# Value copies of the dilated attention: one feature to a DMA issue in place of two

## The chip, the core and the metric

The kernel runs on one core of a Trainium2 chip. A core has five engines that run side by side, each with its own queue of instructions in a fixed order: TensorE (PE, matrix products; its weight loads are shown as PEld), VectorE (DVE), ScalarE (ACT), GpSimd (POOL) and SyncE (SP). In this kernel SP's queue issues nearly all DMA transfers, which are carried out by 16 DMA engines. The metric is the time of one execution on the device, in microseconds; of several runs the median is given.

## What is computed

Four layers follow each other on x, of 2048 rows and 512 columns in bf16: A, B, A, B. Each is `x = x + layer(layernorm(x))`, with 32 heads of 16 features. The A layers are a linear attention with a softmax feature map. The B layers are a sliding attention in which row s looks at the eight rows s, s-2, ..., s-14:

```python
qkv = (x @ wqkv).reshape(B, S, 3, H, Dh)            # H = 32, Dh = 16
idx = pos[:, None] - off[None, :]                   # off = 0, 2, ..., 14
kg, vg = k[:, :, idx_c, :], v[:, :, idx_c, :]       # eight keys and values for each row
logits = einsum("bhsd,hswd->bhsw", q, kg) * Dh ** -0.5   # rows before the start masked
attn = softmax(logits)
o = einsum("bhsw,bhswd->bhsd", attn, vg)
return o.reshape(B, S, D) @ wo
```

The change concerns `vg` in the B layers: how the values reach the engine that multiplies them by `attn`.

## The kernel before

The rows are cut into four blocks of 512. What is called layer 0 and layer 1 below (L in the names) is a pair A, B each, so that there are eight B blocks (two layers of four). Work is recorded as small steps (`step`, L174) under a name of stage and engine. A list written out in the kernel (`_ORDER`, L56) then emits one step after another, so every engine's instructions stand in an order fixed by hand; no scheduler moves them. Buffers come from pools whose slots are written out as well: Vg, prod, pav and Ek share eight large buffers ("big"), so a transfer into one of them may have to wait until an earlier user is done.

One B block goes like this:

- `s_b1` (L919) projects q, k and v with TensorE (L927); ScalarE or VectorE moves the results out of PSUM (L191). The columns of the weight are taken four apart, so partition 4h + dl holds the features 4 dl to 4 dl + 3 of head h, one in each of four chunks of 16 + 512 rows, the 16 being the rows before the block. Such a group of four is what is called one feature below (dl, or q where it is used: 0 to 3). GpSimd fills those 16 (L965, L969).
- `vwr` (L971 to L973) writes V to DRAM, one row of 4 x 528 elements for each of the 128 partitions: row 4h + dl is feature dl of head h.
- `vrep` reads it back four times, shifted: partition 32g + h of Vg receives the row of head h from position 2 + 2g on, 2104 elements of 2 bytes. So the four groups g of 32 partitions hold four of the eight offsets, and the other four are read 8 elements further on. Vg consists of two tiles, k = 0 with dl = 0 and 1, k = 1 with dl = 2 and 3.
- `s_b2` forms the products of q and k on VectorE (prod, L1015), sums them on TensorE (L1022), and makes the softmax: E (L1029), its sum (L1038), its reciprocal (L1043, L1045) and the weights PT (L1050).
- `s_b3` (L1064) takes the features in turn: for q = 0 to 3 VectorE multiplies PT by the window of Vg of feature q (pav, L1077: tile q // 2, half q % 2), TensorE adds over the offsets (L1086), and the sum is moved to oT (L191). In the last two blocks of layer 1 the product of q = 3 is made in two halves of columns.
- `s_out` (L508) multiplies oT by the output weights (L519), adds x (L522 with L529 on ScalarE, or L532 on VectorE), and goes on to the next norm, whose result xn is transposed into xnT, in most blocks by a DMA (L450) on SP's queue.

In each B block SP's queue so has one write of V (vd, L973) and four steps of `vrep`, of two DMAs each. The steps lie at places of their own in the order, with transposes and other blocks' writes between some of them. In the first half of each tile's transfer the groups 0 and 2 come, in the second the groups 1 and 3. The last two blocks of layer 1 are interleaved: both of block 3's steps for k = 0, one of block 2's, both of block 3's for k = 1, and then the other three of block 2's.

A DMA completes on one of eight semaphores, given out in turn; an issue waits until the DMA that had the same one, eight DMAs before, has landed. A pav waits for the DMAs that wrote what it reads.

Of the kernel before, what the change touches and what calls it, by code (L numbers as in the profile page):

```python
# [19 lines left out]
H = 32  # L20
# [3 lines left out]
NB = 4  # L24
# [5 lines left out]
KVW = 16 + TB  # L30
VGW = 3 * KVW + TB + 8
# [97 lines left out]
class _Fast:  # L129
# [789 lines left out]
    def s_b1(self, L, b):  # L919
        nc, add = self.nc, self.step  # L920
        st = "b1_%d%d" % (L, b)
        T = {}
        def mm(i, c):
            xnT = self.xnT["B%d" % L, b]
            T[i, c] = pp = self.ps()
            for k in range(NB):
                nc.tensor.matmul(pp[:], lhsT=self.WB[:, k, i * D + c:(i + 1) * D:NB], rhs=xnT[:, :, k, :],  # L927
                                 start=(k == 0), stop=(k == NB - 1))

        def ev(i, c, dve):  # L930
            if i == 0:
                if (L, b) not in self.QT:
                    self.QT[L, b] = self.med([NB, TB], "QT")
                dst = self.QT[L, b][:, c, :]
            elif i == 1:
                ktile()
                dst = self.K[L, b][:, c, 16:KVW]
            else:
                vtile()
                dst = T["V"][:, c, 16:KVW]  # L940
            self.copy(dve, dst, T[i, c][:])

        def ktile():
            if (L, b) not in self.K:
                self.K[L, b] = self.med([NB, KVW], "K")

        def vtile():
            if "V" not in T:
                T["V"] = self.med([NB, KVW], "V")

        def halo():
            ktile()
            nc.gpsimd.tensor_copy(out=self.K[L, b][:, :, 0:16], in_=self.K[L, b - 1][:, :, TB:KVW])

        def kzero():
            ktile()
            nc.gpsimd.memset(self.K[L, b][:, :, 0:16], 0.0)

        def vzero():
            vtile()  # L960
            nc.gpsimd.memset(T["V"][:, :, 0:16], 0.0)

        def vhalo_in():
            vtile()
            nc.gpsimd.tensor_copy(out=T["V"][:, :, 0:16], in_=self.vh[L, b - 1][:])  # L965

        def vhalo_out():
            self.vh[L, b] = self.sm([NB, 16], "vh", BF16)
            nc.gpsimd.tensor_copy(out=self.vh[L, b][:], in_=T["V"][:, :, TB:KVW])  # L969

        def vwr():  # L971
            self.VD[L, b] = self.dram.tile([P, NB * KVW], BF16, name="vd%d%d" % (L, b))
            nc.sync.dma_start(out=self.VD[L, b][:], in_=T["V"][:].rearrange("p c t -> p (c t)"))  # L973

        def vrep(k, gs):
            if gs[0] == 0:
                if k == 0:
                    self.Vg[L, b] = {}
                self.Vg[L, b][k] = self.big([2, NB * KVW], "Vg")
            n = NB * KVW  # L980
            for g in gs:
                a = self.VD[L, b][2 * k:2 * k + 1, 2 + 2 * g:3 + 2 * g]
                src = bass.AP(a.tensor, a.offset, [[4 * n, H], [n, 2], [1, VGW]])
                nc.sync.dma_start(out=self.Vg[L, b][k][32 * g:32 * g + 32, :, 0:VGW], in_=src)

        if b:
            add(st + "v", "POOL", vhalo_in)
        else:
            add(st + "k", "POOL", kzero)
            add(st + "v", "POOL", vzero)  # L990
        for i in range(3):
            for c in range(NB):
                add(st + "qkv"[i], "PE", mm, i, c)
                self.flex(st + "qkv"[i], ev, i, c)
        if b:
            add(st + "kh", "POOL", halo)
        if b < 3:
            add(st + "v", "POOL", vhalo_out)
        add(st + "v", "SP", vwr)
        for k in range(2):  # L1000
            for gs in ((0, 2), (1, 3)):
                add(st + "v", "SP", vrep, k, gs)

    def s_b2(self, L, b):
        nc, add = self.nc, self.step
# [229 lines left out]
class _Layout:  # L1235
# [6 lines left out]
    def add(self, name, nelem, nbuf=1):  # L1242
        self.regions[name] = (self.off, nelem, nbuf)
        self.off += nelem * nbuf
        return self
# [568 lines left out]
```

## Time and profile before

| | |
|---|---|
| median of 3 runs | 335.52 us (334.93 to 337.06) |
| the profiled execution | 335.42 us |
| its span, first to last instruction | 333.6 us |
| mean granted TensorE clock | 0.988 |
| busy: PE, DVE, ACT, POOL | 309.3, 299.3, 283.4, 20.7 us |
| Vg transfers | 64 issues of 263.0 KB |
| bytes moved by DMA in all | 41.03 MB |

The profile is of one execution. Times in it are microseconds from the span's start. A line such as L1077 is a line of the kernel's source. `out<-in` names the tiles that an instruction writes and reads. In brackets stands how long the engine was idle before an instruction, and what ended that idle time. In the chain of work that ended last, a "DMA" piece lasts from the issue to the landing. For a queue (SPq) the time of a row is that of the issues, not of the transfers.

### The profile page before, as it was taken

The numbers are of one execution on the slowest core, as the hardware profiler recorded it, in microseconds if no ns is written. First come the engines' busy times: TensorE is split into PE (matmuls) and PEld (weight loads), VectorE is DVE, ScalarE is ACT, GpSimd is POOL, SyncE is SP. The second block draws the span as 40 slices with busy tenths as digits, with TensorE's granted clock in tenths as the row PEclk, the third lists the DMA queues.
The fourth block names the chain that finished last, engine by engine and source line by source line (L and its number), as shares of the span: only waits on it lengthen the run. The fifth ranks groups of instructions, "written<-read, shape, count | busy, mean of one in ns | idle before, by whom it ended". The sixth has DMA issues, their size and how long they took to land.

```text
span 333.6 us, 7904 instructions
## 1 busy us (share of the span) xinstructions
PE 309.3 (93%) x3149; PEld 150.2 (45%) x3174; DVE 299.3 (90%) x435; ACT 283.4 (85%) x641; POOL 20.7 (6%) x50
## 2 busy tenths in 40 slices
PE   7999998999999999799999999989999999998590
PEld 3654546445554444244444545634544445433240
DVE  5999996979999986999999899699999999996991
ACT  4999989998898898699999999999999997675270
POOL 4000000000001000000000000000031041300000
PEclk9999999999999999999999999999999999999797
DMA  7948000042735989683841200051527849479642
GB/s 200 336 108 218 26 2 4 2 109 48 166 69 153 179 204 250 168 172 72 211 107 21 45 1 2 6 135 26 142 56 199 184 130 228 159 162 225 132 173 88
DMA packets 42828, 41.03 MB, mean 123 GB/s; under 512 B 27424, under 2 KB 36640, under 8 KB 42784
## 3 DMA queue, kind: packets, MB, share of 16 engines
q1 hardware_dynamic: 42256, 40.44, 49.8%
q8 instruction: 26, 0.43, 0.6%
q14 instruction: 18, 0.15, 0.2%
q10 hardware_dynamic: 528, 0.02, 0.1%
HBM read 27.74 MB, written 6.95 MB: 104 GB/s over the span
## 4 chain that ended last, share of the span: by engine, by line
PE 38%; ACT 23%; DVE 22%; DMA 10%; issue 3%; SPq 1%; DVEq 0%; ACTq 0%
PE ps L927 17%; PE ps L519 7%; DMA Vg<-vd 6%; DVE pav L1077 6%; ACT Eq L705 4%; ACT sqd L539 3%; PE ps L697 2%; DMA xnT<-xn 2%; DVE Ek L650 2%; ACT oT L191 2%; DVE stat L492 2%; PE ps L604 2%; PE ps L1022 2%; ACT xn L445 2%; ACT x L529 2%
## 5 line engine op out<-in xcount | busy, mean ns | idle before, releaser
L927 PE MATMUL ps<-xnT,WB 128*128 128x512 bf16 x384 | 87.3, 380 | 0.5 <-DMA xnT<-xn 0.2
L1077 DVE TENSOR_TENSOR pav<-PT,Vg 128x4096 bf16<-128x4096 bf16 (+1 forms) x34 | 72.2, 2165 | 7.8 <-DMA Vg<-vd 7.4
L1015 DVE TENSOR_TENSOR prod<-QT,K 128x4096 bf16<-128x4096 bf16 x32 | 71.8, 2285 | 0.3
L927 PEld LDWEIGHTS <-WB 128*128 128x128 bf16 x384 | 42.7, 114 | 42.6 <-issue 5.7
L519 PEld LDWEIGHTS <-oT 128*128 128x128 bf16 x256 | 24.3, 99 | 33.4 <-issue 3.9
L191 ACT CAST oT<-ps 128x512 bf16<-128x512 f32 (+1 forms) x55 | 30.2, 588 | 8.8 <-PE ps L1086 8.4
L705 ACT ACTIVATE Eq<-ps 128x512 bf16<-128x512 f32 x64 | 34.9, 615 | 0.3 <-PE ps L697 0.3
L519 PE MATMUL ps<-WoB,oT 128*128 128x512 bf16 x123 | 32.9, 388 | 1.5 <-ACT oT L191 1.1
L598 ACT ACTIVATE Ek<-ps 128x512 bf16<-128x512 f32 x64 | 34.1, 621 | 0.0
L697 PE MATMUL ps<-xnT,WA 128*128 128x512 bf16 x128 | 31.6, 379 | 0.6 <-ACT bs L846 0.3
L539 ACT ACTIVATE sqd<-x 128x512 bf16<-128x512 bf16 x48 | 30.3, 632 | 1.8 <-DVE x L532 0.6
L604 PE MATMUL ps<-WA,xnT 128*128 128x512 bf16 x122 | 30.0, 379 | 0.4
L592 PE MATMUL ps<-WA,xnT 128*128 128x512 bf16 x123 | 30.0, 379 | 0.2
L519 PE MATMUL ps<-WoA,oT 128*128 128x512 bf16 x122 | 29.0, 379 | 0.6 <-ACT oT L191 0.3
L1086 PE MATMUL ps<-pav,indAV 128*32 128x512 bf16 (+1 forms) x272 | 17.5, 373 | 7.8 <-DVE pav L1077 7.8
L532 DVE SCALAR_TENSOR_TENSOR x<-ps,x 128x512 bf16<-128x512 f32 x35 | 23.0, 683 | 0.2 <-PE ps L519 0.2
L529 ACT ACTIVATE x<-ps 128x512 bf16<-128x512 f32 x29 | 16.7, 605 | 6.6 <-PE ps L522 6.6
L191 ACT CAST QT<-ps 128x512 bf16<-128x512 f32 x31 | 18.2, 596 | 3.3 <-PE ps L927 3.3
L445 ACT ACTIVATE xn<-x,nmr,rstd 128x512 bf16<-128x512 bf16 x23 | 18.0, 815 | 1.4 <-DVE nmr L434 1.3
L604 PEld LDWEIGHTS <-xnT 128*128 128x128 bf16 x128 | 12.3, 98 | 15.2 <-issue 0.4
L191 ACT CAST K<-ps 128x512 bf16<-128x512 f32 x31 | 17.9, 595 | 1.1 <-PE ps L927 1.0
L650 DVE TENSOR_TENSOR Ek<-Ek,rk 128x4096 bf16<-128x4096 bf16 (+1 forms) x10 | 18.6, 1860 | 0.2 <-ACT rk L645 0.2
(128 smaller groups left out, 426.5 us busy)
## 6 DMA issues: line engine op xcount, KB each, us to landing
Vg<-vd SPq DMA_DIRECT2D x64, 263.0 KB, 5.7
vd<-V SPq DMA_DIRECT2D x8, 528.0 KB, 3.6
Prho<-rd SPq DMA_DIRECT2D x8, 512.0 KB, 5.7
x<-in_A_x_dram SPq DMA_DIRECT2D x3, 512.0 KB, 8.1
WB<-in_B_wqkv_dram SPq DMA_DIRECT2D x3, 512.0 KB, 9.4
wraw<-in_A_wqkv_dram SPq DMA_DIRECT2D x4, 256.0 KB, 4.0
out_dram<-x SPq DMA_DIRECT2D x8, 128.0 KB, 2.5
out_dram<-x SPq DMA_DIRECT2D x4, 256.0 KB, 2.4
```

The lines of the kernel that those rows point to most:

```text
L191: self.nc.scalar.copy(out=out, in_=in_)
L519: nc.tensor.matmul(y[:], lhsT=oT[:, c, t * P:(t + 1) * P], rhs=Wo()[:, c, :], start=(c == 0), stop=(c == NB - 1 and not onpe))
L539: nc.scalar.activation(out=sqd[:], in_=xb[:, t, :], func=ACT.Square, accum_out=T["ss"][:, t:t + 1])
L592: nc.tensor.matmul(pk[:], lhsT=xnT[:, t, k, :], rhs=self.WA[:, k, D:2 * D], start=(k == 0), stop=(k == NB - 1))
L598: nc.scalar.activation(out=T["E"][:, t, s, :], in_=T["k", t][:], func=ACT.Exp, scale=1.0 - 2.0 * s)
L604: nc.tensor.matmul(pv[:], lhsT=xnT[:, t, k, :], rhs=self.WA[:, k, 2 * D:3 * D], start=(k == 0), stop=(k == NB - 1))
L650: nc.vector.tensor_tensor(out=ev, in0=ev, op=ALU.mult, in1=T["r"][:, 0:m * G, :].unsqueeze(2).to_broadcast([P, m * G, 8, 2]))
L697: nc.tensor.matmul(pq[:], lhsT=self.WA[:, k, hb * P:(hb + 1) * P], rhs=xnT[:, :, k, :], start=(k == 0), stop=(k == NB - 1))
L705: nc.scalar.activation(out=self.Eq[L, b][s][:, :, hb, :], in_=T[hb][:].rearrange("p (t i) -> p t i", t=4), func=ACT.Exp, scale=1.0 - 2.0 * s)
L927: nc.tensor.matmul(pp[:], lhsT=self.WB[:, k, i * D + c:(i + 1) * D:NB], rhs=xnT[:, :, k, :], start=(k == 0), stop=(k == NB - 1))
L1015: nc.vector.tensor_tensor(out=pr[:], in0=QT[:, c:c + 1, :].to_broadcast([P, NW, TB]), in1=win, op=ALU.mult)
L1077: nc.vector.tensor_tensor(out=pv, in0=PT[:, :, lo:lo + n].unsqueeze(1).to_broadcast([P, NB, 2, n]), in1=vw, op=ALU.mult)
```

## The change

Each step of `vrep` now moves one feature (dl) to all four groups of partitions, in the order 0, 2, 1, 3, with four DMAs of 32 rows. Before, a step moved two features to two groups of partitions, with two DMAs of 64 rows. There are still four steps to a block, at the same places in the order, and the two tiles are allocated at the same steps; the rows read and written are the same.

```diff
-        def vrep(k, gs):
-            if gs[0] == 0:
-                if k == 0:
-                    self.Vg[L, b] = {}
-                self.Vg[L, b][k] = self.big([2, NB * KVW], "Vg")
-            n = NB * KVW
-            for g in gs:
-                a = self.VD[L, b][2 * k:2 * k + 1, 2 + 2 * g:3 + 2 * g]
-                src = bass.AP(a.tensor, a.offset, [[4 * n, H], [n, 2], [1, VGW]])
-                nc.sync.dma_start(out=self.Vg[L, b][k][32 * g:32 * g + 32, :, 0:VGW], in_=src)
+        def vrep(dl):
+            if dl == 0:
+                self.Vg[L, b] = {}
+            if dl % 2 == 0:
+                self.Vg[L, b][dl // 2] = self.big([2, NB * KVW], "Vg")
+            for g in (0, 2, 1, 3):
+                a = self.VD[L, b][dl:dl + 1, 2 + 2 * g:3 + 2 * g]
+                src = bass.AP(a.tensor, a.offset, [[4 * NB * KVW, H], [1, VGW]])
+                nc.sync.dma_start(out=self.Vg[L, b][dl // 2][32 * g:32 * g + 32, dl % 2, 0:VGW], in_=src)
...
         add(st + "v", "SP", vwr)
-        for k in range(2):
-            for gs in ((0, 2), (1, 3)):
-                add(st + "v", "SP", vrep, k, gs)
+        for dl in range(4):
+            add(st + "v", "SP", vrep, dl)
```

## The prediction

> **What bounds the kernel now.** I read the page from its top: the busy shares, the chain that ended last, the groups and the DMA issues.
>
> ```profile
> span 333.6 us, 7904 instructions
> ...
> PE 309.3 (93%) x3149; PEld 150.2 (45%) x3174; DVE 299.3 (90%) x435; ACT 283.4 (85%) x641; POOL 20.7 (6%) x50
> ...
> PE 38%; ACT 23%; DVE 22%; DMA 10%; issue 3%; SPq 1%; DVEq 0%; ACTq 0%
> ...
> Vg<-vd SPq DMA_DIRECT2D x64, 263.0 KB, 5.7
> ```
>
> PE, DVE and ACT are all nearly full, so little can be won by less work; what is left is the places where all of them stand still together. The DMA's tenth of the chain is such a place. The view of waits shows VectorE's products of the weights with the gathered value copies (pav) waiting for Vg: 7.4 us in all, three times, 3.4 us the longest.
>
> ```profile
> DVE pav L1077 <- DMA Vg<-vd: 7.4, 3, 3.4
> ```
>
> VectorE's timeline says where:
>
> ```profile
> 121.24 4.49 DVE L1077 TENSOR_TENSOR pav<-PT,Vg 128x4096 bf16<-128x4096 bf16 x2 [1.27 <-DMA Vg<-vd]
> 125.84 0.69 DVE L1050 TENSOR_TENSOR PT<-E,rden 128x1024 bf16<-128x1024 bf16 x1
> 129.28 9.02 DVE L1077 TENSOR_TENSOR pav<-PT,Vg 128x4096 bf16<-128x4096 bf16 x4 [2.75 <-DMA Vg<-vd]
> ...
> 301.14 4.49 DVE L1077 TENSOR_TENSOR pav<-PT,Vg 128x4096 bf16<-128x4096 bf16 x2
> 308.98 13.56 DVE L1077 TENSOR_TENSOR pav<-PT,Vg 128x4096 bf16<-128x4096 bf16 x8 [3.35 <-DMA Vg<-vd]
> ```
>
> Three waits: 1.27 us (block 1 of layer 0, features 2 and 3), 2.75 us (block 0 of layer 0, all four) and 3.35 us (block 3 of layer 1, features 2 and 3). In the other five blocks Vg is there in time. The SP queue's timeline gives the issues behind them and what is queued near them:
>
> ```profile
> 122.23 3.60 SPq L984 DMA_DIRECT2D Vg<-vd  x8
> 128.57 0.34 SPq L973 DMA_DIRECT2D vd<-V  x1
> 135.62 4.42 SPq L984 DMA_DIRECT2D Vg<-vd  x8
> 143.71 12.76 SPq L450 DMA_TRANSPOSE xnT<-xn  x2
> ...
> 252.73 3.62 SPq L984 DMA_DIRECT2D Vg<-vd  x8
> 259.11 4.56 SPq L450 DMA_TRANSPOSE xnT<-xn  x1
> ...
> 293.54 12.18 SPq L984 DMA_DIRECT2D Vg<-vd  x16
> ```
>
> **What the change adds.** 64 issues become 128, each with half the bytes (263.0 KB to 131.5 KB); bytes, row lengths, tiles and every engine's order stay. Two prices are needed: one issue on SP, and one landing.
>
> The issue: eight took 3.60 us, 0.45 each, so sixteen take 7.2, and SP is free 3.6 us later per block. A half-size issue is not in the trace; the extremes of the 64 bound it:
>
> ```profile
> L984 SPq DMA_DIRECT2D Vg<-vd x64: 303/425/1080, 105.5 to 305.4; - x64
> ```
>
> I keep 0.45, as the 128 KB loads of x at the start, the nearest in size, take the same (three in 1.44 us):
>
> ```profile
> 1.32 1.44 SPq L314 DMA_DIRECT2D x<-in_A_x_dram  x3
> ```
>
> The landing: for the eight issued from 122.23 to 125.40 (the last 0.43 before 125.83), the time from issue to landing was
>
> ```profile
> DMA to landing us min/median/max: 3.4/5.8/8.1
> ```
>
> The first landed at 125.6, the eighth at 133.5: seven steps of 1.13 us behind a fixed 3.4 - 1.13 = 2.27. The landings are further apart than the issues (1.13 against 0.45), so the bytes set the pace. Halved, that is 0.565 each, still above 0.45, so a block's last byte lands when it did. Bounds for that step: 0.45 (only the issue limits) and 1.13 (a cost per DMA, whatever its size). I take 0.565, since the x loads of 128 KB landed 3.2 to 3.5 us after issues 0.48 us apart, with no queue growing:
>
> ```profile
> DMA to landing us min/median/max: 3.2/3.3/3.5
> ```
>
> **What it moves.** Before, features 0 and 1 arrive together after DMAs 1 to 4, and 2 and 3 after 5 to 8. Afterwards each feature is complete after its own four half-size DMAs, and in the changed program's order each pav waits for four DMA semaphores of its own. So features 0 and 2 come half a tile's bytes earlier (2.26 us) and 1 and 3 when they did.
>
> *First wait (121.24).* Feature 2 comes 2.3 us earlier, and VectorE had waited only from 119.97 (121.24 - 1.27), so the 1.27 us go. By itself that is worth nothing: the block behind it waits for its own Vg.
>
> *Second wait (129.28).* This row is the chain's:
>
> ```profile
> 123.52 5.54 DMA Vg<-vd
> ```
>
> The fourth DMA landed at 123.52 + 5.54 = 129.06, and pav began 0.22 later. Four half-size ones land at 122.23 + 2.27 + 4 x 0.565 = 126.8, so pav can begin at 127.0, after PT ends at 126.53: 2.3 us earlier. The others then come just in time: 129.0, 131.3 and 133.5 against starts at 129.3, 131.5 and 133.8 (9.02 us for four, 2.25 each). The gain of 2.3 holds to the block's end.
>
> How much of it lasts? The other engines waited there for this pav:
>
> ```profile
> 138.36 0.62 PE L1086 MATMUL ps<-pav,indAV 128*32 128x512 bf16 x8 [1.59 <-DVE pav L1077]
> ...
> 142.32 0.39 PE L519 MATMUL ps<-WoB,oT 128*128 128x512 bf16 x1 [0.85 <-ACT oT L191]
> ```
>
> ```profile
> 138.68 0.30 ACT L427 ACTIVATE lnv<-q,eps_t 128x4 f32<-128x4 f32 x1 [2.10 <-DVE q L551]
> ```
>
> So they can follow by about 2 us (PE idled 1.59 + 0.85, ACT 2.10). What cannot is the transposed xnT issued at 143.71, which PE reads first at 150.56:
>
> ```profile
> 150.56 1.03 PE L697 MATMUL ps<-xnT,WA 128*128 128x512 bf16 x4
> ```
>
> ```profile
> xnT<-xn SPq DMA_TRANSPOSE x1, 5.0
> ```
>
> It landed at 148.7, 1.8 us after the last Vg bytes of block 2 (135.62 + 2.27 + 9.04 = 146.9), whose start hangs on DMA traffic that does not move; and SP now issues until 142.8. From 150.56 that leaves 1.9 us, and I count **1.9** (bounds: 0, if another wait takes its place, and the whole 2.3).
>
> *Third wait (308.98).* From 293.54 SP issues, in this order, block 3's features 0 and 1 (four DMAs), half of block 2's (two), block 3's features 2 and 3 (four), and the other six of block 2. The chain has numbers 2 and 10:
>
> ```profile
> 293.91 3.96 DMA Vg<-vd
> 297.88 10.97 DMA Vg<-vd
> ```
>
> Number 10 landed at 297.88 + 10.97 = 308.85 and ended the wait. Number 8:
>
> ```profile
> 296.73 0.43 SPq L984 DMA_DIRECT2D Vg<-vd  x1
> ```
>
> ```profile
> Vg<-vd SPq DMA_DIRECT2D x1, 263.0 KB, 8.7
> ```
>
> landed at 305.4. Afterwards block 3's feature 2 is complete at number 8's place in the stream of bytes, and feature 3 at number 10's. VectorE ends features 0 and 1 at 305.63, so feature 2 runs 305.7 to 307.9, and feature 3 begins at 308.98 in place of 311.2: **2.3** earlier, with 1.1 us of the wait left. Block 2's feature 0 is there sooner than before, feature 1 at number 12's place; the last needs the last DMA, which lands before 305.72 + 11.0 = 316.7 (no landing in that group took longer) and is wanted at 320.1 - 2.3 = 317.8. From VectorE's last pav on nothing changes.
>
> *Behind the doubled issues.* The write of block 2's V at 128.57 finds SP busy to 129.4, 0.9 us longer; its bytes queue behind Vg's until 133.5 anyway, which hides that. The transpose at 259.11 finds SP busy to 259.9, and PE waits for it:
>
> ```profile
> 259.11 8.12 DMA xnT<-xn
> ```
>
> ```profile
> 267.28 6.20 PE L927 MATMUL ps<-xnT,WB 128*128 128x512 bf16 x28 [0.24 <-DMA xnT<-xn]
> ```
>
> It took 8.12 us against 5.0 above, behind Vg bytes that end at 264.0 either way; they hide the 0.8 us, or else PE stands that much longer. The additional semaphore waits on VectorE are passed while the pav before still runs: nothing (the four in 9.02 us include one that waits for four DMAs already, and no pause).
>
> **Sum:** 1.9 + 2.3 = 4.2 us. The profiled execution took 335.42 (its span is 333.6), the median of the runs shown is 335.52; so 331.2 against the one and **331.3** against the other.
>
> **Rivals.** (a) *Only the end's gain is kept.* Between 140 and 293 us all three engines are full; if ACT or PE cannot take up the 1.9, the time is 335.5 - 2.3 = 333.2. For it: the three shares above; against it: they idled together for this very pav. (b) *The transposes follow the issues.* If the one at 259.11 lands later by the 0.8 us, and (a) holds, 334.0. For it: PE's 0.24 us. (c) *Shorter turns between the groups speed the bytes up.* The groups alternate between halves of the partitions; with turns half as long two DMAs might overlap better, down to 0.45 a step. The second wait then goes entirely (2.75, and the transpose at 143.71 comes 1.8 earlier), the third too (3.35): 329.4. Against it: DMAs at every such change of group land a steady 1.13 apart. [...] (d) *Slower: a DMA costs by its number, not its bytes.* At a step of 0.70 us block 0's feature 3 arrives when it is wanted now (129.28 + 6.77 = 136.05, less 122.23, 2.27 and 0.22, over 16), and at 0.66 block 3's does (311.2 - 293.54 - 2.5, less 1.9 us by which the eight steps from number 2, at 297.87, to number 10 exceeded 8 x 1.13, over 20); from there on the change loses. At 0.85, three quarters of a full DMA's step, block 0 ends 2.3 later and block 2's last feature comes at 293.54 + 4.4 + 27.2 = 325.1, 5.0 later: 342.8; at 1.13 some 356. Against it: the x loads. [...] That the change doesn't do what it says is left out by the order of waits.
>
> **How the numbers follow.** Forecast 0.52 (330.2 to 332.8), (a) 0.20, (b) 0.08, (c) 0.08, (d) 0.12. The range from 329.2 to 336.5 takes in (c), the forecast, (a) and (b), and (d) up to a step of about 0.72. Within 1% means 332.2 to 338.9, about what a measurement here can tell from no change. Faster: (c) and 0.42 of the forecast, 0.50. Slower: nearly all of (d), 0.11. The rest, 0.39.
>
> **What the changed profile would show.** Vg issues x128 of 131.5 KB, sixteen in about 7.2 us, landings 0.57 apart. VectorE's waits for Vg fall from 7.4 us to about 1.5, the last one some 1.1 before block 3's feature 3; pav of block 0 begins about 127.0. PE reads block 1's xnT near 148.7 in place of 150.56, and the last sixteen-DMA group starts near 291.6. Wrong would be: landing steps over 0.66 us, a transposed xnT for which PE waits over 1 us, or pav starting on time and the layers behind it no earlier.

## The result and the profile after

The kernel after takes **327.19 us** (median of four runs, 327.1 to 327.81) against 335.41 for the kernel before on the same chip: a ratio of 0.975, 95% interval 0.9715 to 0.9786. On another chip it was 327.83 against 335.12, a ratio of 0.980 (0.9768 to 0.9833). The forecast was 331.3, its range 329.2 to 336.5: the sign was right, the gain about twice the 4.2 us that were expected. The profiled execution took 327.1 us, with a span of 325.3 (before 335.42 and 333.6).

The page of the kernel after, in the lines that answer to those shown of before (spans, busy time, the chain by engine, the DMA issues):

```profile
span 325.3 us, 8025 instructions
...
PE 309.9 (95%) x3174; PEld 150.0 (46%) x3174; DVE 299.5 (92%) x435; ACT 283.2 (87%) x641; POOL 21.6 (7%) x50
...
PE 38%; ACT 21%; DVE 20%; DMA 7%; issue 6%; SPq 5%; DVEq 0%; ACTq 0%
...
Vg<-vd SPq DMA_DIRECT2D x128, 131.5 KB, 3.4
```

The busy times stand where they were (DVE 299.3, now 299.5); only idle time has gone. The issues are 128 of half the size, as the change says. The view of waits of the kernel after has what is left of VectorE's waits for Vg, 1.2 us of 7.4:

```profile
DVE pav L1075 <- DMA Vg<-vd: 1.2, 2, 0.7
```

VectorE's timeline of the kernel after (start, length, instruction, and in brackets the idle time before it) shows the places:

```profile
119.71 4.49 DVE L1075 TENSOR_TENSOR pav<-PT,Vg 128x4096 bf16<-128x4096 bf16 x2
125.71 2.29 DVE L1075 TENSOR_TENSOR pav<-PT,Vg 128x4096 bf16<-128x4096 bf16 x1 [0.71 <-DMA Vg<-vd]
128.46 6.82 DVE L1075 TENSOR_TENSOR pav<-PT,Vg 128x4096 bf16<-128x4096 bf16 x3 [0.45 <-DMA Vg<-vd]
...
298.52 17.96 DVE L1075 TENSOR_TENSOR pav<-PT,Vg 128x4096 bf16<-128x4096 bf16 x10
```

The first wait is gone, the second is 0.71 + 0.45 in place of 2.75, and the third is gone wholly: the ten products from 298.52 on run without a pause, where two and eight stood 3.35 us apart. The SP queue's timeline of the kernel after has the copies behind them:

```profile
121.56 8.51 SPq L983 DMA_DIRECT2D Vg<-vd  x16
130.18 0.36 SPq L973 DMA_DIRECT2D vd<-V  x1
133.90 7.56 SPq L983 DMA_DIRECT2D Vg<-vd  x16
141.57 3.29 SPq L450 DMA_TRANSPOSE xnT<-xn  x1
...
290.41 16.50 SPq L983 DMA_DIRECT2D Vg<-vd  x32
```

Block 0's copies start 0.67 us sooner than before (121.56 against 122.23), block 2's 1.72 (133.90 against 135.62), the transpose behind them 2.14, the last group 3.13. The view by stretches cuts both executions at the same events: the start of block 0's copies, the end of that block's pavs, PE's first read of the transposed xnT, the start of the last group of copies, the end of the last pav, the end of the span. Its columns are the stretch and its length, the busy time of each engine, the granted clock, the DMA share and GB/s. Of the kernel before:

```profile
122.20:138.30 16.10, 13.34 (x100) 5.70 (x99) 13.21 (x8) 12.96 (x33) 0.66 (x3) 1.00 0.78 196
138.30:150.60 12.30, 11.34 (x80) 5.00 (x82) 11.85 (x13) 10.96 (x28) 0.68 (x2) 1.00 0.87 183
150.60:293.50 142.90, 139.40 (x1467) 67.81 (x1478) 135.81 (x177) 134.20 (x309) 12.32 (x9) 1.00 0.42 101
293.50:322.50 29.00, 23.23 (x184) 9.12 (x188) 25.41 (x16) 16.41 (x37) 0.00 (x0) 0.94 0.79 188
322.50:333.60 11.10, 3.60 (x23) 1.36 (x23) 3.41 (x13) 0.54 (x2) 0.00 (x0) 0.80 0.30 97
```

Of the kernel after:

```profile
121.50:135.30 13.80, 13.54 (x103) 6.03 (x101) 12.50 (x8) 13.22 (x33) 0.95 (x3) 1.00 0.67 205
135.30:147.50 12.20, 11.32 (x80) 4.97 (x81) 11.75 (x11) 10.88 (x28) 0.36 (x2) 1.00 0.90 211
147.50:290.40 142.90, 140.31 (x1479) 67.84 (x1478) 135.44 (x177) 134.18 (x309) 13.25 (x11) 1.00 0.39 101
290.40:316.50 26.10, 22.71 (x188) 8.71 (x188) 25.86 (x19) 16.73 (x37) 0.00 (x0) 1.00 0.74 222
316.50:325.30 8.80, 3.33 (x23) 1.21 (x20) 3.35 (x12) 0.37 (x1) 0.00 (x0) 0.88 0.26 84
```

The ledger, row by row: 0.7 ahead of the first row (the stretch up to it ends at 121.5 in place of 122.2), 2.3 in block 0, 0.1 behind it, nothing in the 142.9 us that follow, 2.9 in the last group, and 2.3 behind the last pav, where no pav and no Vg copy runs any more. They add to 8.3, the difference of the spans. So three questions were open: why block 0 gave 3.0 and kept it, why the last wait went whole, and what the 2.3 us at the end are.

### The profile page after: what moved, and what is told of

It reads as the page before. It is cut to its first block, busy times and chain, and to the rows that moved or that the text cites. A ratio compares the mean times of both kernels' runs of the same rounds, so it can differ in the third digit from the quotient of the medians.

```text
span 325.3 us, 8025 instructions
## 1 busy us (share of the span) xinstructions
PE 309.9 (95%) x3174; PEld 150.0 (46%) x3174; DVE 299.5 (92%) x435; ACT 283.2 (87%) x641; POOL 21.6 (7%) x50
## 4 chain that ended last, share of the span: by engine, by line
PE 38%; ACT 21%; DVE 20%; DMA 7%; issue 6%; SPq 5%; DVEq 0%; ACTq 0%
PE ps L927 15%; PE ps L519 8%; SPq L983 5%; ACT sqd L539 3%; DMA Vg<-vd 3%; DVE pav L1075 3%; DVE prod L1013 3%; DMA vd<-V 3%; ACT Eq L705 3%; PE ps L697 3%; DVE Ek L650 2%; PE ps L604 2%; DVE stat L492 2%; ACT xn L445 2%; ACT oT L191 2%
## 5 line engine op out<-in xcount | busy, mean ns | idle before, releaser
L604 PE MATMUL ps<-WA,xnT 128*128 128x512 bf16 x128 | 30.5, 379 | 0.1
L592 PE MATMUL ps<-WA,xnT 128*128 128x512 bf16 x128 | 30.5, 379 | 0.0
L519 PE MATMUL ps<-WoA,oT 128*128 128x512 bf16 x128 | 29.8, 380 | 0.1
L604 PEld LDWEIGHTS <-xnT 128*128 128x128 bf16 x128 | 12.3, 98 | 15.6 <-issue 1.0
L592 PEld LDWEIGHTS <-xnT 128*128 128x128 bf16 x128 | 12.2, 98 | 14.2 <-issue 0.2
## 6 DMA issues: line engine op xcount, KB each, us to landing
Vg<-vd SPq DMA_DIRECT2D x128, 131.5 KB, 3.4
```

Source lines behind the costliest of these rows:

```text
L519: nc.tensor.matmul(y[:], lhsT=oT[:, c, t * P:(t + 1) * P], rhs=Wo()[:, c, :], start=(c == 0), stop=(c == NB - 1 and not onpe))
L592: nc.tensor.matmul(pk[:], lhsT=xnT[:, t, k, :], rhs=self.WA[:, k, D:2 * D], start=(k == 0), stop=(k == NB - 1))
L604: nc.tensor.matmul(pv[:], lhsT=xnT[:, t, k, :], rhs=self.WA[:, k, 2 * D:3 * D], start=(k == 0), stop=(k == NB - 1))
```

## The experiments

Each kernel ran beside the kernel before on its own chip. "Last pav" is the end of VectorE's last pav in the profile, "tail" the time from there to the end of the span.

**Split alone.** The kernel before, each issue cut into its two features, the bytes in their old order:

```diff
-                src = bass.AP(a.tensor, a.offset, [[4 * n, H], [n, 2], [1, VGW]])
-                nc.sync.dma_start(out=self.Vg[L, b][k][32 * g:32 * g + 32, :, 0:VGW], in_=src)
+                for d in range(2):
+                    src = bass.AP(a.tensor, a.offset + d * n, [[4 * n, H], [1, VGW]])
+                    nc.sync.dma_start(out=self.Vg[L, b][k][32 * g:32 * g + 32, d, 0:VGW], in_=src)
```

> The kernel before with each Vg issue cut into its two features, one after the other (group 0: feature 0, feature 1; group 2: the same; then groups 1 and 3). 128 issues of 131.5 KB as in the changed kernel, but the bytes come in the order of before: feature 0 is complete with the 7th of a tile's eight, feature 1 with the 8th. Theory O (only the order of the bytes matters, 0.565 us a step): features 0 and 2 come 0.6 us earlier than before; about 334.5 us, or 332.5 if the shorter end of the program (below) belongs to the number of issues. Theory S (a half-size DMA lands sooner by itself, as the changed kernel's first landings of 2.3 us in place of 3.3 suggest): waits of VectorE for Vg fall from 7.4 to about 4 us, the write of V in front of the second wait lands 0.7 us earlier; 330 to 331 us. Theory E (2 us at the end of the program come from where the instructions of SP lie, as SP has 63 more): the stretch from the last pav to the end is 8.8 us, not 11.1.

Measured: 332.18 us, ratio 0.9907 (0.9875 to 0.9939). VectorE's timeline of this kernel:

```profile
120.89 4.49 DVE L1078 TENSOR_TENSOR pav<-PT,Vg 128x4096 bf16<-128x4096 bf16 x2 [0.94 <-DMA Vg<-vd]
128.87 4.50 DVE L1078 TENSOR_TENSOR pav<-PT,Vg 128x4096 bf16<-128x4096 bf16 x2 [2.69 <-DMA Vg<-vd]
133.90 4.49 DVE L1078 TENSOR_TENSOR pav<-PT,Vg 128x4096 bf16<-128x4096 bf16 x2 [0.53 <-DMA vd<-V]
...
307.93 13.56 DVE L1078 TENSOR_TENSOR pav<-PT,Vg 128x4096 bf16<-128x4096 bf16 x8 [1.74 <-DMA Vg<-vd]
```

Half the size by itself leaves block 0's wait as it was (2.69) and halves the last one (1.74 in place of 3.35). Its last pav ends at 321.49, 1.05 sooner than before; most of its 3.1 us come from the tail, 8.97 in place of 11.07. The time is near the 332.5 that theory O has with the shorter end. What the change gains beyond this kernel comes from the order in which features become whole, and from the order of the partition groups, which this kernel changes too; the next two runs tell them apart.

**The groups in turn.** The kernel after, with the partition groups taken 0, 1, 2, 3; and the kernel before, with its pairs taken so:

```diff
-            for g in (0, 2, 1, 3):
+            for g in (0, 1, 2, 3):
```

```diff
-            for gs in ((0, 2), (1, 3)):
+            for gs in ((0, 1), (2, 3)):
```

> The changed kernel with the four groups of a feature in the order 0, 1, 2, 3 in place of 0, 2, 1, 3, so that two DMAs in turn write the same half of the partitions. Every feature is complete at the same place in the stream. Theory O (order of bytes alone): as the changed kernel, 327.2 us. Theory H (DMAs in turn overlap because they write different halves of the partitions): steps grow from about 0.5 to between 0.57 and 1.0 us (a half-size DMA alone adds 1.0 us to the landing), VectorE waits 3 us or more for Vg, 329 to 335 us.

> The kernel before with the groups of a step paired 0, 1 and 2, 3 in place of 0, 2 and 1, 3: whole-size DMAs, two in turn to the same half of the partitions. Theory O: as before, 335.4 us, steps of 1.13 us. Theory H: steps of 1.3 to 2.0 us, and 338 to 350 us.

Measured: 329.32 us, ratio 0.9823 (0.978 to 0.9866), and 337.31, ratio 1.0069 (1.0045 to 1.0092). The kernel with the pairs loses 2.0 us to the kernel before on the same chip (337.31 against 335.29). The one with the groups 0, 1, 2, 3 loses 1.5 to 2.1 to the kernel after, which ran on other chips (329.32 against 327.83 and 327.19), and 1.1 to 1.3 by the end of the last pav (317.76 against 316.63 and 316.48). The landings in block 0 say why: a half-size step (first to last landing, by the number of half-size steps between them) is 0.56 us before and 0.57 after, but 0.62 (groups) and 0.61 (pairs) in these two, and 0.62 in the split kernel, which also sends two features of one group one behind the other. Neighbours in the same half of the partitions cost 9% of the pace in block 0. For the pairs that is less than theory H had put, 1.22 us a whole-size step in place of 1.3 to 2.0. Read against the split kernel, which shares its pace and its chip, the kernel with groups 0, 1, 2, 3 prices the order of the features alone: 332.18 - 329.32 = 2.9 us. The alternation is worth another 1 to 2, less certain since it is compared across chips.

**Layer 0 alone, and the last two blocks alone.** The kernel before, with the new issues in some of its blocks:

```diff
-        for k in range(2):
-            for gs in ((0, 2), (1, 3)):
-                add(st + "v", "SP", vrep, k, gs)
+        if L == 0:                      # in the other kernel: L == 1 and b >= 2
+            for dl in range(4):
+                add(st + "v", "SP", vrep1, dl)
+        else:
+            for k in range(2):
+                for gs in ((0, 2), (1, 3)):
+                    add(st + "v", "SP", vrep, k, gs)
```

> The new issues in layer 0's four blocks alone, layer 1's as before. If the parts of the gain add: block b0 of layer 0 ends 3.0 sooner (near 135.3), nothing of that is lost through layer 1, the last group keeps its wait of about 3.4, and the last pav ends near 319.5; with the tail of 11.1 the time is 332.4, with one of 8.8 it is 330.1 (SP has 32 instructions more than before, half of the change's 63). Rival (the gain of block b0 is taken back by TensorE before the end, as waits elsewhere): the last pav ends near 322.5, 335.4 or 333.1.

> The new issues in the last two blocks of layer 1 alone, the other six as before. If the parts add: block b0 of layer 0 ends where it did, near 138.3, the last group starts near 293.5 and has no wait, and the last pav ends 2.9 sooner, near 319.6; time 332.5 with the tail of 11.1, 330.2 with 8.8 (SP has 15 instructions more). Rival (the wait at the end goes only when the last group starts 3 us sooner): a wait of 1 to 3 us stays, the last pav ends at 321 or later, 334 or more.

Measured: 331.71 us, ratio 0.9899 (0.9859 to 0.994), and 329.74, ratio 0.9851 (0.9815 to 0.9886). VectorE's timeline of the kernel with layer 0 alone:

```profile
125.96 2.29 DVE L1091 TENSOR_TENSOR pav<-PT,Vg 128x4096 bf16<-128x4096 bf16 x1 [0.80 <-DMA Vg<-vd]
129.40 6.82 DVE L1091 TENSOR_TENSOR pav<-PT,Vg 128x4096 bf16<-128x4096 bf16 x3 [1.15 <-DMA Vg<-vd]
...
306.59 13.56 DVE L1091 TENSOR_TENSOR pav<-PT,Vg 128x4096 bf16<-128x4096 bf16 x8 [2.73 <-DMA Vg<-vd]
```

and of the kernel with the last two blocks alone:

```profile
129.10 9.10 DVE L1091 TENSOR_TENSOR pav<-PT,Vg 128x4096 bf16<-128x4096 bf16 x4 [2.53 <-DMA Vg<-vd]
...
301.16 17.96 DVE L1091 TENSOR_TENSOR pav<-PT,Vg 128x4096 bf16<-128x4096 bf16 x10
```

In the first, block 0 ends at 129.40 + 6.82 = 136.22, 2.1 sooner than before, and the last pav at 320.15, 2.4 sooner: nothing is lost on the way through layer 1. In the second, block 0 stands as before, the last group starts at 293.50 as before, and the wait is gone all the same: the last pav ends at 319.12, 3.4 sooner. The two add to 5.8, and the kernel after has 322.54 - 316.48 = 6.1 (5.9 in its second profile, 316.63). The parts add.

**The early write.** Block 0's copies wait for the write of its V, which is issued at 115.06 behind block 1's copies and lands at 122.2, though the records of V's writers end at 102.7 at the latest. This one step is moved ahead in SP's written order (here as SP has them in layer 0), in the kernel before to 107.4 and in the kernel after to 109.2; in another kernel, made of the one after, to 103.5, ahead of the first copies of block 1:

```diff
 vd of b1
 Vg of b1, features 0 and 1
+vd of b0
 a transpose of xn
 Vg of b1, features 2 and 3
-vd of b0
 Vg of b0
```

> The kernel before, with the write of b0's V of layer 0 (issued at 116.5 behind b1's eight copies, though its data are there at 102.7) moved ahead of b1's second half of copies. Theory S (block b0's wait hangs on when its copies start, too): they start near 117 instead of 122.2, have landed near 128, the wait of 2 to 3 us ahead of b0's pavs goes in the old order as well, block b0 ends about 3 us sooner; time 332 to 333 with the old tail. Rival O (only the order of the bytes helps; the copies of b0 then collide with those of b1): b1's pavs wait longer by what b0's gain, 335 or more.

> The kernel after, with the write of b0's V of layer 0 moved to 108.9 (from 116.5, behind b1's second half of copies). Theory S (what is left of b0's wait, 0.71 and 0.45, hangs on the start of b0's copies): they start near 117, both waits go, and since b1's third pav has 1.6 us of room now, little comes back there; block b0 ends up to 1.2 sooner, time 326.0 to 326.5. Rival (collision, as it was seen in the kernel before with the early write, where b1's third pav lost 1.1 of b0's gain): b1's second half lands 2 to 3 us later, its pavs wait 1 us, time 327 or more.

> The kernel after, with the same write moved further, to 102.9, right behind the write of b1's V and ahead of b1's first half of copies, whose features 0 and 1 land 6 us ahead of their pavs. Theory S: as with the write at 108.9, but b1's second half doesn't meet it: 326.0. Rival (collision): b1's copies as a whole are pushed back by the write's 3 us, the transposed xnT at 110.4 with them, and the second half waits as well: 327 or more.

Measured: the kernel before so changed 333.16, ratio 0.9953 (0.993 to 0.9976); the kernel after 326.44, ratio 0.9748 (0.9725 to 0.9771), and 326.25, ratio 0.9748 (0.9724 to 0.9772). VectorE's timeline of the kernel before with the early write:

```profile
122.33 4.50 DVE L1075 TENSOR_TENSOR pav<-PT,Vg 128x4096 bf16<-128x4096 bf16 x2 [2.28 <-DMA Vg<-vd]
127.71 9.10 DVE L1075 TENSOR_TENSOR pav<-PT,Vg 128x4096 bf16<-128x4096 bf16 x4
```

and of the kernel after with it (at 109):

```profile
119.94 4.50 DVE L1073 TENSOR_TENSOR pav<-PT,Vg 128x4096 bf16<-128x4096 bf16 x2
125.32 9.06 DVE L1073 TENSOR_TENSOR pav<-PT,Vg 128x4096 bf16<-128x4096 bf16 x4
```

In the old order block 0's wait goes too, but block 1 pays 1.0 of it back (2.28 us in place of 1.27): the write's bytes come ahead of its second half. Block 0 so ends 1.5 us sooner (136.81 against 138.30), not the 3 of theory S, and the time lies between the two theories. In the new order block 1's third pav has room, and no wait for Vg is left, as theory S had it. Side by side on one chip, the kernel after and the one with the write at 109:

> The kernel after itself, beside the same kernel with the early write on one chip. Theory S (the 1.16 us of b0's wait that the change left are worth their length, since nothing behind block b0 takes them back): 327.2 here, 326.4 there. Rival (the transposed xnT or TensorE takes them back): both 327.2, or less than 0.3 apart.

> The kernel after with the write of b0's V at 108.9 once more. Theory S: 0.8 below the kernel after on the same chip (as the last pavs of the two profiles stand, 315.67 against 316.48). Rival: less than 0.3 below.

Measured: 327.83 (ratio to before 0.980, 0.9768 to 0.9833) and 326.76 (0.9754, 0.9734 to 0.9773). They are 1.07 us apart in the medians, 0.76 in the last pav (316.63 and 315.87); the two intervals still overlap. The profiles agree with the theory that what block 0 saves is passed on; that the version is faster than the kernel after is likely, not settled by these intervals.

**The tail.** In SP's records (semaphore instructions and a branch, which the timeline leaves out) the kernel before stands still behind its last branch: the branch ends at 329.00, one instruction follows at 329.46, the next at 331.78. In the kernel after the branch ends at 322.60, and they follow at 323.06, 323.15 and 323.22. Two kernels tried what decides that. One cuts a load in a branch that this input never takes into 64, which adds 63 issues that are not executed (SP still has 200 instructions ahead of its last branch); the other cuts layer B's output weight loads, near 32 us, into 67:

```diff
-    nc.sync.dma_start(out=x_sb[:], in_=A_x.rearrange("b (p j) d -> p (b j) d", p=P))
+    for j in range(64):
+        w = NJ * D // 64
+        nc.sync.dma_start(out=x_sb[:].rearrange("p j d -> p (j d)")[:, j * w:(j + 1) * w],
+                          in_=A_x.rearrange("b (p j) d -> p (b j d)", p=P)[:, j * w:(j + 1) * w])
```

```diff
-            nc.sync.dma_start(out=self.WoB[c * H:(c + 1) * H, :, :], in_=wo_v[c])
+            cut = list(range(0, H, 2)) + [H - 1] * (c > 0) + [H]
+            for lo, hi in zip(cut[:-1], cut[1:]):
+                nc.sync.dma_start(out=self.WoB[c * H + lo:c * H + hi, :, :], in_=wo_v[c][lo:hi])
```

> The kernel before with 63 more SP instructions in the general path, which is not executed (its load of x is written as 64 DMAs in place of one): every executed instruction is the same, and only the place of the program's end behind that path moves, by as many SP instructions as the change adds. Theory E (2 us at the end come from where the instructions lie): last pav to end 9 us in place of 11.1, 333.4 us. Theory O (the end is shorter because the stores or the waits are): as before, 335.4 us.

> The kernel before, with the four loads of layer B's output weights (issued near 32 us, first read in layer B) cut into 67 of a row or two each: the same bytes, 63 more SP instructions in a stretch where SP is idle, nothing else touched. Theory F (the 2.3 us at the end hang on where SP's executed instructions stand when its last branch is taken, not on the Vg copies): the last pav ends where it did, near 322.5, the tail from there to the end of the span falls from 11.1 to 8.8, time near 333.1. Rival (the tail is shorter because of the Vg copies themselves): the tail stays 11.1 and the time 335.4.

Measured: 335.06 us, ratio 0.9992 (0.997 to 1.0014), with the stall still there (2.76 us); and 338.49, ratio 1.0114 (1.0056 to 1.0171), slower where 333.1 was expected. SP's timeline of the second says why it is slower:

```profile
30.24 33.01 SPq L401 DMA_DIRECT2D WoB<-in_B_wo_dram  x50
...
63.79 11.64 SPq L401 DMA_DIRECT2D WoB<-in_B_wo_dram  x17
75.54 1.30 SPq L826 DMA_DIRECT2D rd<-rho  x2
```

Its issues took 0.66 us each, not the 0.45 that I had counted on, ran to 75.4, and pushed the write of rho from 68.60 to 75.54. But the stall is gone and its tail is 8.91. So a gentler cut, into 17 (`range(0, H, 8)`, one more for the last):

> The kernel before, with layer B's four output weight loads cut into 17 (of eight rows, the last of seven and one): 13 more SP instructions, 8 us more of issues near 32 us where SP then idles until 68. Theory F (the 2.3 us of the end hang on where SP's executed instructions stand at its last branch; 15 more were enough in the last-two-blocks kernel): nothing moves up to the last pav, near 322.5, the tail falls from 11.1 to 8.8, time 333.1. Rival (the tail needs the new copies): 335.4, tail 11.1.

Measured: 333.86 us, ratio 0.9968 (0.9953 to 0.9982), a gain of 0.75 (0.6 to 1.6) where 2.3 was expected. To see how much the tail varies by itself, the kernel before was profiled again:

> The kernel before itself, profiled a second time, since its runs lie between 333.7 and 337.1 and the one profiled was at 335.4. Theory F1 (the stall of SP behind its last branch is about the same in every execution): the stall is 2.2 to 2.3 us again, the tail 11.1, whatever the time. Rival F2 (the stall varies, and is shorter in executions near the median of 334.6, which is why the kernel with a few fine loads gained 0.75 in its median and not 2.3): a profile near 334.5 shows a stall of about 1 us and a tail of 10; at 335.4 or above, 2.2 or more.

Measured: 335.04 us, ratio to its other runs 0.9995 (0.9978 to 1.0012); the profiled execution took 334.12, with a stall of 2.30 us and a tail of 9.97. Neither theory holds as put: the stall is the same in the two profiles (2.32 and 2.30), the tail is not, because SP comes to its last branch 6.46 us behind the last pav in one execution (329.00) and 5.37 in the other (327.82). What compares is the time from the branch's end to the end of the span, in us:

| kernel | SP instructions ahead of the branch | stall | branch to end |
|---|---|---|---|
| before; its second profile | 200 | 2.32; 2.30 | 4.62; 4.60 |
| pairs 0,1 and 2,3 | 200 | 2.19 | 4.49 |
| load cut in the branch not taken | 200 | 2.76 | 4.81 |
| before, early write | 201 | 2.76 | 4.67 |
| a few fine loads | 213 | none | 2.91 |
| last two blocks alone | 215 | none | 2.88 |
| layer 0 alone | 232 | none | 3.27 |
| split alone; groups 0,1,2,3 | 263 | none | 3.24; 2.72 |
| many fine loads | 263 | none | 2.76 |
| after; its second profile | 263 | none | 2.69; 3.33 |
| after, early write: at 109, twice; at 103 | 264; 263 | none | 2.70, 3.36; 2.71 |

The view by stretches shows the two parts of the tail, up to the branch's end and behind it, of the kernel before

```profile
322.50:329.00 6.50, 3.60 (x23) 1.36 (x23) 3.41 (x13) 0.54 (x2) 0.00 (x0) 1.00 0.42 138
329.00:333.60 4.60, 0.00 (x0) 0.00 (x0) 0.00 (x0) 0.00 (x0) 0.00 (x0) 0.52 0.12 39
```

and of the kernel with a few fine loads:

```profile
322.80:329.00 6.20, 3.32 (x23) 1.21 (x20) 3.34 (x12) 0.37 (x1) 0.00 (x0) 0.96 0.33 109
329.00:331.90 2.90, 0.00 (x0) 0.00 (x0) 0.00 (x0) 0.00 (x0) 0.00 (x0) 0.50 0.20 66
```

All engines are idle in the last row of each, 4.60 us long against 2.90. The kernels with 200 or 201 instructions stall (2.19 to 2.76 us), those with 213 or more do not, whether the additional ones are Vg copies or weight loads. So about 1.3 to 1.9 us of the change's gain (4.62 against 3.33 and 2.69) have nothing to do with when Vg arrives. In the medians the few fine loads gave only 0.75. Their last pav was 0.2 later (322.77), so that 1.5 should have come (4.62 - 2.91 - 0.2), which lies near the upper end of the interval of 0.6 to 1.6; why the median shows half of it stays open. What SP waits for in the stall is not shown: the trace of the kernel before has 8 KB packets of an instruction queue (q14) at 330.05 and 330.15, in the midst of the stall, 1.1 us behind the branch, but the kernel after has such packets as well, 1.1 to 1.5 us behind its branch, and does not stall. No kernel here has between 202 and 212 instructions, and none shows why the stall is gone with more.

## Why the prediction was right or wrong

**What held.** The places of the three waits and what ends them; 0.45 us for an issue (sixteen in 7.26 to 7.56, near the 7.2 expected, though 8.51 in block 0); a landing step of 0.57 in block 0 where 0.565 was put, so that a half-size DMA costs by its bytes here and rival (d) is out; the transpose at 259.11, which is hidden (it lands at 263.93 in place of 267.23); and that ACT and PE can take up block 0's gain, which rival (a) doubted: the stretch of 142.9 us has the same length in both kernels, and layer 0 alone passed on its 2.1 as 2.4. That the first wait is worth nothing by itself was not tried alone.

**Second wait: the cap was wrong.** I counted 2.3 us and let 1.9 last, because the transposed xnT hung "on DMA traffic that does not move". It moved. Block 0 gave 3.0 in the profile of after and 2.1 with layer 0 alone (the two differ in the wait left ahead of the second pav, 0.45 and 1.15). The sizes: the first half-size copy landed 2.34 us after its issue, not 2.27 + 0.565 = 2.84, as the first full one had landed at 3.42; so the fixed part is 1.8 with this step, not 2.27, and pav began at 125.71 instead of 127.0. Block 0's copies started 0.67 sooner (121.56), of which 0.2 is the whole timeline's offset (VectorE's first pav 115.14 against 115.35). And block 2's write landed at 133.81 in place of 135.53, its copies started 1.72 sooner and the transpose 2.14 sooner. The transpose landed at 146.95 in place of 148.69, and PE read xnT at 147.53: 3.0 sooner where I had allowed 1.9, and sooner than it could have with the old landing.

**Third wait: the size was wrong.** I kept 1.1 of the 3.35 us, since block 3's feature 3 was to come at number 10's old place, 15.32 us after the group's start. That landing was late by itself: number 9 had landed at 13.04, and the step of 2.28 us between them is about twice those ahead of it (about 1.2, one of 1.54). The bytes did not stand still meanwhile. The view by stretches has 231 GB/s (its last figure) for these 2.28 us of the kernel before:

```profile
306.58:308.86 2.28, 0.52 (x12) 0.03 (x4) 0.00 (x0) 1.66 (x4) 0.00 (x0) 1.00 1.06 231
```

A full-size copy is 64 packets of 4208 bytes in the trace. The 640th packet of the group, the bytes of ten copies, had ended at 13.09 us; number 10 landed 2.2 us behind that, and I carried its landing over as if the bytes had needed it. With half-size issues the 640th packet had ended at 12.39 (after) and 11.91 (last two blocks alone), and the twentieth copy landed at 14.04 and 13.45, 1.3 and 1.9 us sooner than 15.32. So the lag behind the bytes was shorter, 1.5 to 1.7 us, and the bytes themselves came faster: 201 GB/s from the group's first issue to its last landing before, 220 after and 229 with the last two blocks alone. Why a landing lags so far, and why the smaller copies came faster here, stays open. The last two blocks alone, whose group starts at the old 293.50, lost the whole wait: 3.4, not 2.3. The forecast had put rival (c)'s faster bytes at 0.08, and at the end it was partly so, while block 0's pace stayed at 0.57.

**"From VectorE's last pav on nothing changes."** This failed: 2.3 us went there in the profiles, of which 1.9 between SP's last branch and the end (4.62 and 2.69), for something that none of my steps contained: with 63 more instructions on SP the stall of 2.32 us was gone. The row for those last 4.6 us of the kernel before, with every engine idle, would have pointed at it.

Put together: 2.1 to 3.0 us where 1.9 was put, 2.9 to 3.4 where 2.3 was, and 2.3 where nothing was. The range's low end, 329.2, lay just under rival (c)'s 329.4, which was worked out with the old tail. Less the 1.9 us behind the branch that rival would stand at 327.5, about what came, but by luck: it had steps of 0.45 us, and block 0's were 0.57.

## What to carry to other kernels

When one consumer needs a whole slice, send the slice's parts one behind the other, and let neighbours alternate between halves of the partitions: the order of completion gave 2.9 us here and the alternation 1 to 2, at the same bytes. Before capping a gain by a transfer "that does not move", ask what starts that transfer; and before taking a landing over as a price, see how many bytes had moved by then, since the landing can lag behind them (by 1.5 to 2.2 us here). Look at the stretch behind the last useful instruction too: 1.3 to 1.9 us of the gain lay there, with 263 instructions in one queue in place of 200.

## What the runs showed of the hardware

**The clock of the last group was lower where VectorE waited in it.** In the stretch of the last group VectorE waits 1.7 to 3.5 us for Vg in nine of the profiles, and the granted clock there is 0.94 in five of them and 0.88 in four; in the seven profiles without that wait it is 1.00. The length of the wait does not say which of the two it is: the kernel before has 0.94 with 3.35 us and 0.88 in its second profile with 3.18, and layer 0 alone has 0.88 with 2.73. The row of that stretch, of the kernel with layer 0 alone,

```profile
291.40:320.20 28.80, 23.95 (x183) 9.11 (x185) 25.83 (x18) 15.88 (x36) 0.00 (x0) 0.88 0.76 183
```

and of the kernel with the last two blocks alone:

```profile
293.50:319.10 25.60, 22.51 (x185) 8.66 (x187) 25.36 (x16) 16.72 (x37) 0.00 (x0) 1.00 0.75 226
```

PE's busy time there is 22.5 to 22.7 us at 1.00, 23.1 to 23.8 at 0.94 and 23.9 to 24.2 at 0.88: 0.4 to 1.7 us more where there is a wait. In the kernel before the clock's records have 0.50 from 312.16 to 315.57, behind that wait, and eight of TensorE's products over the offsets (L1086), from 312.46 on, took 0.62 us there; in the kernel after, whose clock is at 1.00 up to 323.26, the same eight took 0.40 (from 306.40). So a wait that goes may give back a little more than its length, an estimate from these times; how much of the gain this makes was not measured apart.

**Two DMAs in the same half of the partitions in a row landed slower.** In block 0 a half-size step takes 0.61 to 0.62 us against 0.56 to 0.57, 9% more, whether the DMAs have 263.0 or 131.5 KB. In the four later groups of eight or more copies it is 5 to 7% at 263.0 KB (the pairs against the kernel before) and 1 to 15% at 131.5 KB (the groups 0, 1, 2, 3 against the kernel after).

**The first DMA of a group gained more from half the size than the steady pace suggests.** In block 0 it landed 2.34 us after its issue at 131.5 KB and 3.42 at 263.0 KB, 1.08 apart, in the last group 2.42 and 3.15, 0.73 apart; in the stream of block 0 behind it the same bytes take 0.57.
